# Linear attention into a GELU layer: the feature map as a minimum of two branches, and the first batch's v casts moved ahead

## The chip, the cores and the metric

The kernel runs on one core of a Trainium2 chip. The metric is the device time of one execution in microseconds (us). The engines of the core run side by side and meet through semaphores: TensorE (PE; its weight loads are listed as PEld), VectorE (DVE), ScalarE (ACT), GpSimd (POOL) and SyncE (SP), which here only issues DMA transfers.

## The reference

Two parts follow one another. The first is linear attention over 8 batches and 8 heads, with 576 tokens and 64 features a head; the second is a two-layer network with a tanh-approximated GELU over all 4608 tokens (512 to 2048 to 512 features).

```
def phi(x):
    return np.where(x > 0, x, np.exp(x) - 1.0) + 1.0
q_p, k_p = phi(q), phi(k)
kv  = np.einsum('bhsd,bhse->bhde', k_p, v)
z   = np.sum(k_p, axis=2)
num = np.einsum('bhsd,bhde->bhse', q_p, kv)
den = np.einsum('bhsd,bhd->bhs', q_p, z)[..., None] + 1e-06
x   = (num / den), tokens x (heads * 64)
h   = x @ w_in
g   = 0.5 * h * (1.0 + np.tanh(c * (h + 0.044715 * h * h * h)))
out = g @ w_out
```

The feature map phi is exp(x) for x up to 0 and x + 1 above. Everything is given and returned in 32-bit floats; the kernel multiplies in bf16.

## The kernel before

**Tiling.** The 576 tokens of a batch are 512 "main" tokens, on 128 partitions with C = 4 tokens ("chunks") in each, and 64 "rest" tokens; the rests of two batches share one tile. q, k and v of a batch are loaded as fp32 tiles of 128x2048 in the order head, chunk, feature (`load_main`, line 63). For the matrix products the feature map's result is wanted in the order chunk, head, feature (`k_p`, `q_p`), so that two heads of one chunk are a block of 128 columns.

**Feature map.** ACT writes e = exp(x) in bf16, in the order of the load (`exp_main`, lines 164 to 167; for the first batch and its rests line 341 and `exp_rest_half`). DVE then clamps e to 1 in place (line 171) and computes max(x, 0) + e for each of the four chunks, with the result in chunk order (`phi_into`, lines 169 to 178). `phi_of`, `phi_rest` and `phi_rest_half` are the same for whole tiles, whole rests and half a rest.

**Attention of a batch.** v is cast to bf16 next to a column of ones (`cast_v`, line 202, and `cast_vr`, line 208). `kv_mm` (line 213) sums kv and z over the chunks and the rest in PSUM; `kv_evac` (line 234) copies them out to a block-diagonal tile `kvbd`. q_p is transposed: on PE for the first two batches (`transpose_q`, line 332, and `tq`, line 555), by DMA transposes issued by SP for the others (lines 455 and 608). `nab_mm` (line 251) multiplies by `kvbd`, `nab_evac` divides, and the result x is transposed again into `xt`.

**Network.** For each batch j, `first_half` makes 16 blocks m of h on PE (`first_mm`, line 298, 4 products each) with GELU on ACT, and `second_half` (line 703) makes the output on PE (line 718, 64 products), which ACT or DVE copy out. A ninth turn handles the rests of all batches.

**Order.** The order on every engine is written out by hand. The prologue (lines 339 to 405) does batch 0 step by step; `keep_warm` issues products on a zero tile so that PE stays busy. From then on `at(half, j, slot, fn)` puts the preparation of later batches between the products of earlier ones.

**Weights and buffers.** Loads of q, k, v and of the weights share one pool of six fp32 buffers (`pld`, tag `ld`), so a load waits until the buffer's former tile has been read. SP issues them in one queue: k and q of batch 0, the first half of the k and v rests, v of batch 0, the first two quarters of w_in, k of batch 1, the rest of w_in, then w_out in four blocks with q and v of batch 1 between them. POOL casts w_in (line 149) and most of w_out (line 156) to bf16 after they land. The second half of j = 0 takes the output tiles in turns, so that its first 16 products need only the first block of w_out.

**The lines that matter for the prologue.** The exps of k and q by halves of the heads (line 341), their maps (line 346), four transposes and copies of q (ACT, lines 348 and 354), the v casts, and the kv products in two groups h of four heads. Before group 0, ACT casts heads 0 to 3 of v; between the groups, DVE casts heads 4 and 5 and ACT heads 6 and 7 (lines 357 to 359).

Of the kernel before, what the change touches and what calls it, by code (L numbers as in the profile page):

```python
# [9 lines left out]
BF16 = mybir.dt.bfloat16  # L10
AF = mybir.ActivationFunctionType
ALU = mybir.AluOpType
# [3 lines left out]
def kernel(  # L16
# [12 lines left out]
    nc = tc.nc  # L29

    B, H, S, D = q.shape
    d_model, d_ff = moe_w_in.shape
    P = 128
    C = 4
# [12 lines left out]
    pe = ctx.enter_context(tc.tile_pool(name="pe", bufs=1))  # L47
# [52 lines left out]
    ld = {}  # L100
# [43 lines left out]
    def gelu_table():  # L144
        nc.scalar.preload_act_table_set("gelu_apprx_tanh_and_others")  # L145
# [15 lines left out]

    phi = {}

    def exp_main(name, b):
        e = pe.tile([P, H, C * D], BF16, name=name + "_e")
        nc.scalar.activation(e, ld[name, b], AF.Exp)  # L166
        return e

    def phi_into(xp, x, e, hs):

        nc.vector.tensor_scalar(e[:, hs], e[:, hs], 1.0, None, op0=ALU.min)  # L171
        xv = x.rearrange("p h (c d) -> p c h d", d=D)
        ev = e.rearrange("p h (c d) -> p c h d", d=D)
        for c in range(xp.shape[1]):
            nc.vector.scalar_tensor_tensor(  # L175
                xp[:, c, hs, :], xv[:, c, hs, :], 0.0, ev[:, c, hs, :],
                op0=ALU.max, op1=ALU.add,
            )

    def phi_of(x, e, name):  # L180
        xp = pphi.tile([P, x.shape[2] // D, H, D], BF16, name=name)
        phi_into(xp, x, e, slice(0, H))
        return xp

    def phi_rest(name, m):
        x = ld[name, m]
        e = pe.tile([P, H, D], BF16, name=f"{name}_e{m % 2 if name == 'qr' else ''}")
        nc.scalar.activation(e, x, AF.Exp)
        return lambda: phi.__setitem__((name, m), phi_of(x, e, name + "_p"))

    def exp_rest_half(name, e, s):
        r = slice(REST * s, REST * (s + 1))
        nc.scalar.activation(e[r], ld[name, 0][r], AF.Exp)

    def phi_rest_half(name, e, s):
        r = slice(REST * s, REST * (s + 1))
        nc.vector.tensor_scalar(e[r], e[r], 1.0, None, op0=ALU.min)
        nc.vector.scalar_tensor_tensor(
            phi[name, 0][r, 0], ld[name, 0][r], 0.0, e[r], op0=ALU.max, op1=ALU.add
        )  # L200

    def cast_v(b, fn, s=slice(0, H)):
        fn(  # L203
            out=vps[b % 2][:, s, :, 0:D],
            in_=ld["v", b][:, s].rearrange("p h (c d) -> p h c d", d=D),
        )

    def cast_vr(m, halves=(0, 1)):
        for s in halves:
            r = slice(REST * s, REST * (s + 1))  # L210
            nc.vector.tensor_copy(out=vrs[m % 2][s][r, :, 0:D], in_=ld["vr", m][r])

    def kv_mm(b, i, kv_ps, at_i=None):
        i_ps = i if at_i is None else at_i
        kp = phi["k", b].rearrange("p c h d -> p c (h d)")
        kr = phi["kr", b // 2].rearrange("p c h d -> p c (h d)")
        dst = kv_ps[:, i_ps // 2, 2 * E * (i_ps % 2) : 2 * E * (i_ps % 2) + 2 * E]
        for c in range(C):
            nc.tensor.matmul(  # L219
                dst,  # L220
                lhsT=kp[:, c, P * i : P * (i + 1)],
                rhs=vps[b % 2][:, 2 * i : 2 * i + 2, c, :],
                start=(c == 0),
                stop=False,
            )
# [70 lines left out]
    gs, hs = {}, {}  # L296
# [18 lines left out]
    ke = pe.tile([P, H, C * D], BF16, name="k_e")  # L315
    qe = pe.tile([P, H, C * D], BF16, name="q_e")
    kre = pe.tile([P, H, D], BF16, name="kr_e")
# [7 lines left out]
    def keep_warm(n):  # L325
        w_ps = ps_ho.tile([P, 512], FP32, name="w_ps", tag="ho")
        for _ in range(2 * n):
            nc.tensor.matmul(w_ps[:, 0:252], lhsT=warm[:, 0:P], rhs=warm)  # L328

    halves = (slice(0, 4), slice(4, 8))  # L330

    def transpose_q(i, copy):
        src = q_src(0)
        t_ps = ps_ho.tile([P, C, 2, P], BF16, name="t_ps", tag="ho")
        for c in range(C):
            nc.tensor.transpose(t_ps[:, c, 0, :], src(c, i), ident)
        copy(out=qt[:, :, i, :], in_=t_ps[:, :, 0, :])

    for n, e in (("k", ke), ("q", qe)):
        for s in halves:  # L340
            nc.scalar.activation(e[:, s], ld[n, 0][:, s], AF.Exp)
    exp_rest_half("kr", kre, 0)
    keep_warm(36)
    for n, xp, e in (("k", kp, ke), ("q", qp, qe)):
        for s in halves:
            phi_into(xp, ld[n, 0], e, s)
    for i in range(2):
        transpose_q(i, nc.scalar.copy)
# [44 lines left out]
    keep_warm(1)  # L393
    tx0(1)
    ke1 = exp_main("k", 1)
    kre1 = pe.tile([P, H, D], BF16, name="kr_e")
    exp_rest_half("kr", kre1, 1)
    gelu_table()
    nab0(3)
# [122 lines left out]
    def plan_second():  # L522

        b = 1
        box = {}

        def exps():
            box["q"] = pe.tile([P, H, C * D], BF16, name="q_e")
            for s in halves:
                nc.scalar.activation(box["q"][:, s], ld["q", b][:, s], AF.Exp)  # L530
            gelu_table()

        def phis():
            phi["q", b] = pphi.tile([P, C, H, D], BF16, name="q_p")
            for s in halves:
                phi_into(phi["q", b], ld["q", b], box["q"], s)
# [257 lines left out]
```

## Time and profile before

| what | value |
|---|---|
| median of four runs | 297.69 us (295.9 to 298.21) |
| the profiled execution, own time | 297.55 us |
| its span, first to last instruction | 295.8 us |
| granted TensorE clock | 1.000 |
| PE busy | 285.7 us, 97% |
| ACT busy | 159.7 us, 54% |
| DVE busy | 130.1 us, 44% |
| POOL busy | 37.1 us, 13% |
| DVE clamp, 128x2048 (line 171) | 13 times, 811 ns (k) and 689 ns (q) on average |
| DVE max and add, 128x512 (line 175) | 28 for k at 746 ns, 24 for q at 686 ns |
| ACT exp, 128x2048 (line 166) | 13 times, about 1.9 us |
| DVE cast of v, 128x2048 (line 203) | 7 times, 1223 ns |
| first FFN product begins | 21.28 us |

A busy share is an average over the whole span. Which engine sets the end is read from the chain of waits and from the list of who waited for whom; idle time of an engine that nobody waits for costs nothing. Matmuls are pipelined, so that their single durations overlap: 64 products of 128x512 take about 13.8 us of PE, not 64 times the 379 ns listed for one.

### The profile page before, as it was taken

What the parts mean: (1) busy time and instruction counts of PE and PEld (TensorE: products, weight loads), DVE (VectorE), ACT (ScalarE), POOL (GpSimd) and SP (SyncE); (2) the same over time, 40 slices, a digit from 0 to 9 for tenths busy, and PEclk for the clock granted to TensorE, in tenths of its full rate; (3) what the DMA queues carried; (4) which work ended last, traced back from release to release, by engine and by line L of the source; (5) the groups of instructions that cost most, each with busy time, mean ns of one, the idle gap of its engine ahead of it and who ended that gap; (6) DMA issues with size and microseconds to landing.
All of it is one profiled execution on the core that took longest, in us unless ns stands there. A gap on an engine that the chain in (4) does not pass through costs nothing.

```text
span 295.8 us, 4289 instructions
## 1 busy us (share of the span) xinstructions
PE 285.7 (97%) x1669; PEld 149.2 (50%) x1698; DVE 130.1 (44%) x244; ACT 159.7 (54%) x222; POOL 37.1 (13%) x56
## 2 busy tenths in 40 slices
PE   8979999999999999999999999999999999999995
PEld 6756445644565444544455445544544444444443
DVE  2868555327689578244624493437142000000002
ACT  4649943579955762658256935683551066017500
POOL 8046567500001500000000000000000000000000
PEclk9999999999999999999999999999999999999999
DMA  7999999993399999637924696203331110021032
GB/s 246 330 365 406 397 371 379 299 371 109 83 319 285 170 299 322 159 74 231 334 90 68 203 335 144 53 20 112 100 55 36 71 71 2 0 86 56 2 71 72
DMA packets 64260, 53.24 MB, mean 180 GB/s; under 512 B 31728, under 2 KB 57584, under 8 KB 64240
## 3 DMA queue, kind: packets, MB, share of 16 engines
q1 hardware_dynamic: 60816, 41.82, 49.3%
q10 hardware_dynamic: 2464, 8.52, 7.4%
q0 software_dynamic: 960, 2.62, 3.8%
q8 instruction: 13, 0.21, 0.3%
q14 instruction: 7, 0.06, 0.1%
HBM read 36.70 MB, written 9.44 MB: 156 GB/s over the span
## 4 chain that ended last, share of the span: by engine, by line
PE 79%; DMA 12%; DVE 4%; issue 2%; ACT 1%; SPq 0%; POOL 0%; DVEq 0%
PE o_ps L718 39%; PE h_ps L301 33%; DMA w_st<-in_moe_w_out_dram 4%; DMA q_x<-in_q_dram 3%; DMA w_st<-in_moe_w_in_dram 3%; PE n_ps L253 3%; PE kv_ps L219 2%; DMA qt<-q_p 2%; PE o_ps L687 1%; DVE q_p L175 1%; DVE kvbd L242 1%; DVE k_p L175 1%; PE t_ps L276 1%; PE kv_ps L226 1%; SPq L67 0%
## 5 line engine op out<-in xcount | busy, mean ns | idle before, releaser
L718 PE MATMUL o_ps<-w_out_sb,g 128*128 128x512 bf16 x545 | 123.7, 379 | 1.2 <-POOL w_out_sb L156 0.4
L301 PE MATMUL h_ps<-xt,w_in_sb 128*128 128x512 bf16 (+1 forms) x535 | 118.8, 364 | 0.8
L675 ACT ACTIVATE g<-h_ps 128x512 bf16<-128x512 f32 x144 | 83.8, 598 | 47.8 <-PE h_ps L301 45.2
L718 PEld LDWEIGHTS <-g 128*128 128x128 bf16 x560 | 54.1, 98 | 63.2 <-issue 0.7
L301 PEld LDWEIGHTS <-w_in_sb 128*128 128x128 bf16 x612 | 57.7, 98 | 54.7 <-issue 0.5
L733 ACT COPY o_sb<-o_ps 128x512 f32<-128x512 f32 x18 | 10.6, 586 | 57.1 <-PE o_ps L718 56.8
L731 DVE COPY o_sb<-o_ps 128x512 f32<-128x512 f32 x17 | 11.7, 688 | 62.4 <-PE o_ps L718 62.3
L265 DVE TENSOR_TENSOR x<-n_ps,r 128x512 bf16<-128x512 f32 x36 | 24.9, 692 | 1.2
L175 DVE SCALAR_TENSOR_TENSOR k_p<-k_x,k_e 128x512 bf16<-128x512 f32 (+1 forms) x36 | 22.0, 674 | 0.3
L175 DVE SCALAR_TENSOR_TENSOR q_p<-q_x,q_e 128x512 bf16<-128x512 f32 (+1 forms) x40 | 21.5, 601 | 0.3
L242 DVE CAST kvbd<-kv_ps 64x260 bf16<-64x260 f32 (+1 forms) x16 | 6.6, 410 | 28.3 <-PE kv_ps L226 28.2
L263 DVE RECIPROCAL r<-n_ps 128x8 f32<-128x8 f32 x36 | 7.4, 206 | 25.3 <-PE n_ps L253 25.3
L171 DVE TENSOR_SCALAR k_e<-k_e 128x2048 bf16<-128x2048 bf16 (+1 forms) x9 | 6.6, 731 | 23.7 <-ACT k_e L166 19.1
L328 PE MATMUL w_ps<-warm 128*128 128x252 bf16 x94 | 13.3, 304 | 1.1 <-DVE warm L127 1.1
L253 PEld LDWEIGHTS <-qt 128*128 128x128 bf16 x128 | 9.7, 98 | 8.7 <-issue 1.1
L301 PE MATMUL h_ps<-xt_rest,w_in_sb 128*128 128x512 bf16 x63 | 13.9, 379 | 0.1
L253 PE MATMUL n_ps<-kvbd,qt 128*128 128x130 bf16 x128 | 12.7, 221 | 1.2 <-DMA qt<-q_p 0.6
L166 ACT ACTIVATE k_e<-k_x 128x2048 bf16<-128x2048 f32 x7 | 13.4, 1911 | 0.4 <-DMA k_x<-in_k_dram 0.4
L219 PEld LDWEIGHTS <-k_p 128*128 128x128 bf16 x128 | 9.7, 97 | 6.8 <-issue 1.4
L203 DVE CAST vp<-v_x 128x2048 bf16<-128x2048 f32 (+1 forms) x8 | 9.0, 1122 | 9.3 <-DMA v_x<-in_v_dram 9.3
L219 PE MATMUL kv_ps<-vp,k_p 128*128 128x130 bf16 x128 | 12.2, 220 | 0.9 <-DVE vp L203 0.8
L145 ACT ACT_TABLE_LOAD x8 | 10.3, 1283 | 3.8 <-DVE o_sb L731 3.8
(58 smaller groups left out, 147.4 us busy)
## 6 DMA issues: line engine op xcount, KB each, us to landing
out_dram<-o_sb ACTq DMA_DIRECT2D x16, 512.0 KB, 3.6
k_x<-in_k_dram SPq DMA_DIRECT2D x7, 1024.0 KB, 6.0
v_x<-in_v_dram SPq DMA_DIRECT2D x7, 1024.0 KB, 12.1
q_x<-in_q_dram SPq DMA_DIRECT2D x6, 1024.0 KB, 9.3
w_st<-in_moe_w_out_dram SPq DMA_DIRECT2D x4, 1024.0 KB, 11.7
w_st<-in_moe_w_in_dram SPq DMA_DIRECT2D x3, 1024.0 KB, 8.8
q_x<-in_q_dram SPq DMA_DIRECT2D x4, 512.0 KB, 10.3
k_x<-in_k_dram SPq DMA_DIRECT2D x2, 512.0 KB, 4.2
```

The lines of the kernel that those rows point to most:

```text
L145: nc.scalar.preload_act_table_set("gelu_apprx_tanh_and_others")
L166: nc.scalar.activation(e, ld[name, b], AF.Exp)
L175: nc.vector.scalar_tensor_tensor(xp[:, c, hs, :], xv[:, c, hs, :], 0.0, ev[:, c, hs, :], op0=ALU.max, op1=ALU.add,)
L219: nc.tensor.matmul(dst, lhsT=kp[:, c, P * i : P * (i + 1)], rhs=vps[b % 2][:, 2 * i : 2 * i + 2, c, :], start=(c == 0), stop=False,)
L253: nc.tensor.matmul(n_ps[rows, i // 2, 2 * E * (i % 2) : 2 * E * (i % 2) + 2 * E], lhsT=qt_c[:, i, rows], rhs=kvbd[:, i, :], skip_group_che ...
L265: nc.vector.tensor_tensor(x, n_v[:, :, :, 0:D], r[:, :, :, None].to_broadcast([P, 2, 4, D]), op=ALU.mult,)
L301: nc.tensor.matmul(h_ps[:, tok], lhsT=w_in_sb[:, c, P * m : P * (m + 1)], rhs=xt[:, c, tok], start=(c == 0), stop=(c == KM - 1), skip_grou ...
L328: nc.tensor.matmul(w_ps[:, 0:252], lhsT=warm[:, 0:P], rhs=warm)
L675: nc.scalar.activation(gs[j][:, i, :], ps, AF.Gelu_apprx_tanh)
L718: nc.tensor.matmul(o_pss[t], lhsT=g[:, m, P * t : P * (t + 1)], rhs=w_out_sb[:, m, :], start=(m == 0), stop=(m == MM - 1),)
L731: nc.vector.tensor_copy(dst, o_ps)
L733: nc.scalar.copy(dst, o_ps)
```

## The change

The feature map is written as min(exp(x), max(x + 1, 1)), which is the same function: below 0 the maximum is 1 and exp is smaller; above 0 exp(x) is larger than x + 1. Each map is now two DVE operations over all chunks instead of one clamp and an operation per chunk: `phi_line` computes max(x + 1, 1) from the loaded fp32 tile and writes bf16 in chunk order, and `phi_min` takes the minimum with e, in place. So that both inputs of the minimum lie in the same order, ACT writes exp in chunk order (`exp_into`), and the tiles for e have the shape chunk, head, feature.

In the prologue, ACT's cast of v's heads 0 to 3 and the casts between the two kv groups are replaced by four casts ahead of both groups: DVE takes heads 0, 1, 4 and 5, ACT heads 2, 3, 6 and 7. The copy of the last transposed block of q (i = 3) goes from ACT to DVE. The first call of `keep_warm` issues 66 products instead of 72.

```
+    def by_chunk(x):
+        return x.rearrange("p h (c d) -> p h c d", d=D)
+
+    def exp_into(e, x, hs=slice(0, H)):
+        nc.scalar.activation(
+            e[:, :, hs, :].rearrange("p c h d -> p h c d"), by_chunk(x[:, hs]), AF.Exp
+        )
+
     def exp_main(name, b):
-        e = pe.tile([P, H, C * D], BF16, name=name + "_e")
-        nc.scalar.activation(e, ld[name, b], AF.Exp)
+        e = pe.tile([P, C, H, D], BF16, name=name + "_e")
+        exp_into(e, ld[name, b])
         return e

-    def phi_into(xp, x, e, hs):
-
-        nc.vector.tensor_scalar(e[:, hs], e[:, hs], 1.0, None, op0=ALU.min)
-        xv = x.rearrange("p h (c d) -> p c h d", d=D)
-        ev = e.rearrange("p h (c d) -> p c h d", d=D)
-        for c in range(xp.shape[1]):
-            nc.vector.scalar_tensor_tensor(
-                xp[:, c, hs, :], xv[:, c, hs, :], 0.0, ev[:, c, hs, :],
-                op0=ALU.max, op1=ALU.add,
-            )
+
+    def phi_line(xp, x, hs=slice(0, H)):
+        nc.vector.tensor_scalar(
+            xp[:, :, hs, :].rearrange("p c h d -> p h c d"), by_chunk(x[:, hs]),
+            1.0, 1.0, op0=ALU.add, op1=ALU.max,
+        )
+
+    def phi_min(xp, e, hs=slice(0, H)):
+        nc.vector.tensor_tensor(
+            xp[:, :, hs, :], xp[:, :, hs, :], e[:, :, hs, :], op=ALU.min
+        )
...
     def phi_rest_half(name, e, s):
         r = slice(REST * s, REST * (s + 1))
-        nc.vector.tensor_scalar(e[r], e[r], 1.0, None, op0=ALU.min)
-        nc.vector.scalar_tensor_tensor(
-            phi[name, 0][r, 0], ld[name, 0][r], 0.0, e[r], op0=ALU.max, op1=ALU.add
-        )
+        phi_line(phi[name, 0][r], ld[name, 0][r])
+        phi_min(phi[name, 0][r], e[r])
...
     for n, e in (("k", ke), ("q", qe)):
         for s in halves:
-            nc.scalar.activation(e[:, s], ld[n, 0][:, s], AF.Exp)
+            exp_into(e, ld[n, 0], s)
     exp_rest_half("kr", kre, 0)
-    keep_warm(36)
+    keep_warm(33)
     for n, xp, e in (("k", kp, ke), ("q", qp, qe)):
         for s in halves:
-            phi_into(xp, ld[n, 0], e, s)
+            phi_line(xp, ld[n, 0], s)
+            phi_min(xp, e, s)
     for i in range(2):
         transpose_q(i, nc.scalar.copy)
     keep_warm(5)
     phi_rest_half("kr", kre, 0)
-    cast_v(0, nc.scalar.copy, halves[0])
     cast_vr(0, (0,))
     for i in range(2, NP):
-        transpose_q(i, nc.scalar.copy)
+        transpose_q(i, nc.scalar.copy if i == 2 else nc.vector.tensor_copy)
     keep_warm(2)
     for h in range(2):
-        if h == 1:
-            cast_v(0, nc.vector.tensor_copy, slice(4, 6))
-            cast_v(0, nc.scalar.copy, slice(6, 8))
+        cast_v(0, nc.vector.tensor_copy, slice(4 * h, 4 * h + 2))
+        cast_v(0, nc.scalar.copy, slice(4 * h + 2, 4 * h + 4))
+    for h in range(2):
         kv_ps = ps_a.tile([P, 2, 512], FP32, name="kv_ps", tag="a")
         for i in range(2):
             kv_mm(0, 2 * h + i, kv_ps, i)
...
```

`phi_of`, `phi_rest`, `exp_rest_half` and the exps and maps of batch 1's q call the new functions in the same way.

More of the change, by code (lines that the diff above doesn't have):

```diff
@@ L162 @@
     phi = {}
+    def by_chunk(x):
[4 more added lines that the diff above has]
+        )
     def exp_main(name, b):
-        e = pe.tile([P, H, C * D], BF16, name=name + "_e")
-        nc.scalar.activation(e, ld[name, b], AF.Exp)
-        return e
-    def phi_into(xp, x, e, hs):
-        nc.vector.tensor_scalar(e[:, hs], e[:, hs], 1.0, None, op0=ALU.min)
-        xv = x.rearrange("p h (c d) -> p c h d", d=D)
-        ev = e.rearrange("p h (c d) -> p c h d", d=D)
-        for c in range(xp.shape[1]):
-            nc.vector.scalar_tensor_tensor(
-                xp[:, c, hs, :], xv[:, c, hs, :], 0.0, ev[:, c, hs, :],
-                op0=ALU.max, op1=ALU.add,
-            )
+        e = pe.tile([P, C, H, D], BF16, name=name + "_e")
+        exp_into(e, ld[name, b])
+        return e
+    def phi_line(xp, x, hs=slice(0, H)):
[7 more added lines that the diff above has]
+        )
     def phi_of(x, e, name):
         xp = pphi.tile([P, x.shape[2] // D, H, D], BF16, name=name)
-        phi_into(xp, x, e, slice(0, H))
+        phi_line(xp, x)
+        phi_min(xp, e)
         return xp
@@ L186, in phi_rest @@
         x = ld[name, m]
-        e = pe.tile([P, H, D], BF16, name=f"{name}_e{m % 2 if name == 'qr' else ''}")
-        nc.scalar.activation(e, x, AF.Exp)
+        e = pe.tile([P, 1, H, D], BF16, name=f"{name}_e{m % 2 if name == 'qr' else ''}")
+        exp_into(e, x)
         return lambda: phi.__setitem__((name, m), phi_of(x, e, name + "_p"))
@@ L192, in exp_rest_half @@
         r = slice(REST * s, REST * (s + 1))
-        nc.scalar.activation(e[r], ld[name, 0][r], AF.Exp)
+        exp_into(e[r], ld[name, 0][r])
     def phi_rest_half(name, e, s):
         r = slice(REST * s, REST * (s + 1))
-        nc.vector.tensor_scalar(e[r], e[r], 1.0, None, op0=ALU.min)
-        nc.vector.scalar_tensor_tensor(
-            phi[name, 0][r, 0], ld[name, 0][r], 0.0, e[r], op0=ALU.max, op1=ALU.add
-        )
+        phi_line(phi[name, 0][r], ld[name, 0][r])
+        phi_min(phi[name, 0][r], e[r])
     def cast_v(b, fn, s=slice(0, H)):
@@ L313, in first_mm_early @@
         first_mm(j, m, hs[j, m], slice(0, MAIN // 2))
-    ke = pe.tile([P, H, C * D], BF16, name="k_e")
-    qe = pe.tile([P, H, C * D], BF16, name="q_e")
-    kre = pe.tile([P, H, D], BF16, name="kr_e")
+    ke = pe.tile([P, C, H, D], BF16, name="k_e")
+    qe = pe.tile([P, C, H, D], BF16, name="q_e")
+    kre = pe.tile([P, 1, H, D], BF16, name="kr_e")
     kp = pphi.tile([P, C, H, D], BF16, name="k_p")
@@ L395 @@
     ke1 = exp_main("k", 1)
-    kre1 = pe.tile([P, H, D], BF16, name="kr_e")
+    kre1 = pe.tile([P, 1, H, D], BF16, name="kr_e")
     exp_rest_half("kr", kre1, 1)
@@ L527, in exps @@
         def exps():
-            box["q"] = pe.tile([P, H, C * D], BF16, name="q_e")
+            box["q"] = pe.tile([P, C, H, D], BF16, name="q_e")
             for s in halves:
-                nc.scalar.activation(box["q"][:, s], ld["q", b][:, s], AF.Exp)
+                exp_into(box["q"], ld["q", b], s)
             gelu_table()
@@ L535, in phis @@
             for s in halves:
-                phi_into(phi["q", b], ld["q", b], box["q"], s)
+                phi_line(phi["q", b], ld["q", b], s)
+                phi_min(phi["q", b], box["q"], s)
         def cast_vs():
```

## The prediction

> **What bounds the kernel now.** I read the page's busy shares first, then the chain of waits in order of time, then TensorE's own waits, then the table of stretches and the timeline at the two places where the chain leaves TensorE. TensorE (PE) is busy for 97% of the span, and this sets the scale: a faster VectorE (DVE, 44%) can bring nothing except where PE waits. The chain (start, length, what) leaves PE for long in two places. This is the first:
>
> ```profile
> 16.93 0.39 PE kv_ps L219 x4
> ...
> 17.40 8.13 DMA w_st<-in_moe_w_in_dram
> 25.53 12.54 DMA w_st<-in_moe_w_out_dram
> 38.12 1.25 POOL w_out_sb L156
> 39.41 3.61 PE o_ps L718 x16
> ```
>
> The prologue's attention ends its kv products at 17.4 us; from there the chain runs through weight loads until PE goes on at 39.41. PE is not idle all this time: from 21.28 it computes the first half of batch 0's FFN. PE's waits (total, times, longest) say how much it lost:
>
> ```profile
> PE kv_ps L219 <- DVE vp L203: 0.8, 1, 0.8
> PE n_ps L253 <- DMA qt<-q_p: 0.6, 1, 0.6
> PE t_ps L276 <- DVE x L265: 0.6, 2, 0.4
> PE o_ps L718 <- POOL w_out_sb L156: 0.4, 1, 0.4
> ```
>
> The first and third lie in the prologue; the fourth (0.44 us before 39.41) and the second (0.59 us before 101.84) lie behind transfers. The stretches show what the early transfers are bound by (stretch and its length; PE, PEld, DVE, ACT, POOL busy; clock; DMA share; GB/s):
>
> ```profile
> 28.00:30.00 2.00, 2.00 (x11) 0.92 (x10) 1.97 (x2) 1.85 (x5) 2.00 (x2) 1.00 1.05 394
> 38.00:40.00 2.00, 1.56 (x8) 0.62 (x7) 1.63 (x3) 1.39 (x3) 1.88 (x2) 1.00 1.09 366
> 130.00:140.00 10.00, 9.95 (x52) 4.46 (x52) 4.85 (x10) 7.18 (x8) 0.00 (x0) 1.00 0.63 181
> ```
>
> In steps of half a microsecond the DMA share is never under 1.00 from 6 to 42 us: the 16 engines are full, so the second w_out block lands near 38.1 however early the engines are. After 105 us PE is full too (9.95 of 10).
>
> **What the Trainium skill says.** "VectorE: DVE Perf Modes", section on the perf-mode tier table: over 2048 elements in SBUF an fp32 `tensor_scalar` takes 1227 ns and a bf16 `tensor_tensor` 1224 ns. The trace agrees on one-input fp32 work (the v casts, 1223 ns); it has no bf16 `tensor_tensor` from SBUF. "SBUF — State Buffer", section Who interferes with whom: GpSimd (POOL) and a DVE operation with two SBUF inputs, or in a two-port mode, block each other. The trace agrees: four k_p operations took 4.18 us from 25.08 beside POOL casts, and 2.50 us from 86.85 with POOL idle. "TensorE: Matmul & The Clock Gate", section Why this matters for your kernels: a PE gap of more than about 3 us lowers the clock. The granted clock here is 1.000; no gap so long occurs, so no trace shows it.
>
> **The change, part by part.**
>
> *Feature map.* For 128x2048 elements, before, one `tensor_scalar` and four `scalar_tensor_tensor`: the k of batch 3 holds DVE from 86.13 to 89.26, 3.13 us. After, an fp32 `tensor_scalar` (nearest row, the v cast: 1.22) and a bf16 `tensor_tensor`. For the latter I bound it by 0.69 us (the row of the bf16 `tensor_scalar`) and 2.33 us (one element at a time: 128x256 took 0.418 and 128x512 0.692, so 1.07 ns an element) and take the page's 1.22. With the 0.04 us that stand between dependent operations in the trace and the 0.08 us by which the next one overlaps, the sum is 1.22 + 0.04 + 1.22 - 0.08 = 2.40: 0.73 us less. There are 13 such maps, so some 9.5 us of DVE time; a rest's map (128x512) gains about 0.2. Nearly all of it lies beside a full PE and is worth nothing. The new first operation does not need exp, so it can run while exp does; the minimum then waits for exp as the old clamp did, with the same operations queued behind it.
>
> *Exp by chunk.* ScalarE (ACT) writes the same elements in runs of 64. The nearest row, its v cast with a gap after every 64, takes 1.05 us for 1024 against 1.057 for exp: cost 0. If scattered writing cost a tenth, two ACT exps would be 0.2 us longer in the prologue, hidden as what follows.
>
> *Prologue.* For 1024 elements I interpolate the DVE casts (0.411 at 512, 1.223 at 2048): 0.68 us for either new operation. The second half of q lands at 10.73; the line part runs to 11.43 while exp runs to 11.81, the minimum from 11.84 to 12.52. Before, q_p was done at 13.73: 1.2 us saved. Behind it on DVE: k's rest (2 x 0.41), the v rest cast 0.41, the moved qt copy 0.42, two v casts of 0.41 each, so about 14.9. On ACT: the exps to 12.33, three copies to about 13.8, two v casts of 0.62 to about 15.0. The v casts, now all ahead of the kv copies, leave no wait between the two kv groups (before: 0.8 and 0.2 us of PE). The last kv product moves from 17.39 to about 15.7 and the first FFN product from 21.28 to about 19.6: 1.6 us, or 1.0 if the second half of v, first read at 15.86 in this trace, is late. Six warm-up matmuls less only let the transposes start earlier. The first w_in cast (17.26, about 1.0 us) is in time.
>
> *What is late next.* PE then asks for m = 6 and 8 at about 25.1 and 26.9. The w_in casts on POOL follow landings at about 23.4 and 25.9, and the DVE work on batch 1's k, now starting at about 23.0 rather than 23.5, can push one back by a two-port operation (1.2): PE loses some 0.4 us. It still comes to the end of the 16 products on the first w_out block at 38.97 - 1.6 + 0.4, about 37.8, and waits for the cast of the second block, which waits for its landing at 38.1. So the gain becomes a wait of about 1.4 us, up from 0.44. What is left of it: at 38.12 the POOL cast took 1.25 us beside DVE's q_p (37.36 to 39.63). The first half of q's line now runs before exp (34.01 to 36.01) and the map ends near 36.9, so the cast should take its undisturbed 1.04: minus 0.21 us.
>
> *Batch 3.* The second place in the chain:
>
> ```profile
> 89.35 1.14 DVE vp L203
> 90.49 0.61 DVE q_e L171
> ...
> 95.78 6.01 DMA qt<-q_p
> 101.84 0.41 PE n_ps L253 x4
> ```
>
> And SyncE's queue (SPq) in the timeline there:
>
> ```profile
> 91.88 5.12 SPq L455 DMA_TRANSPOSE qt<-q_p  x4
> ```
>
> Four DMA transposes issue back to back, 1.28 us each, the first when chunk 0 of q_p exists (91.12 + 0.69 = 91.81). After, all chunks come at once: 86.13 + 2.40 (k) + 1.14 (v cast, as in the chain) + 1.22 + 0.04 + 1.22 = 92.15. DVE is 0.7 us ahead after k and loses that by no longer handing over by chunk. The issues move by plus 0.3 us, and so does the landing at 101.79, on which PE waits. Bounds: with a 0.69 us minimum (k and q) minus 0.7 us, with 2.33 plus 2.5. Earlier batches transpose on PE or wait for kv; later ones have microseconds of room (SyncE from 114.17, PE asks at 123.7).
>
> *Sum*, against the profiled execution's own 297.55 us (span 295.8 and 1.75 around it): -0.2 + 0.3 = +0.1, so 297.6. The median of the four runs is 297.69, 0.14 above that execution.
>
> **The rivals.**
>
> *A, the prologue's gain is kept* (296.0): the second w_out block lands earlier with the rest. For it: SyncE's queue shows waits for slots ahead of w_out loads (1.8 us on a POOL cast, 1.3 us on k_p), which now end earlier. Against: the DMA share of at least 1.00; an earlier issue then only lengthens a queue. Sum: 297.55 - 1.6 + 0.1 = 296.05.
>
> *B, slower, by the minimum at one element per cycle*: 2.33 us instead of 1.22. Its place is batch 3, twice, ahead of the transposes; the price is 2 x 1.11 on top of the forecast, 299.8. It decides from the point where the minimum exceeds about 1.1 us, since the slack of qt is already negative. For: no row of this trace shows the fast form of an operation with two SBUF inputs. Against: both inputs are bf16 in dense runs, and the page prices just this.
>
> *C, the longer wait at 39 us cools PE's clock*: 1.4 to 2 us idle is under 3, but the waits of other engines could stretch it. An estimate from that page (section What's actually happening: an idle or busy window of about 3.4 us, half clock when cold): plus 1.7, 299.3.
>
> **How the numbers follow.** Forecast 0.58, A 0.20, B 0.14, C 0.08. What a measurement here can tell from no change is about 0.5%, 1.5 us. Of the forecast's 0.58, 0.54 lie within it and 0.02 on either side; so faster 0.22, same 0.54, slower 0.24. The range takes in A with a little below and C: 295.7 to 299.3; outside are B and the tails, under 0.2. The forecast's own range, from the bounds at batch 3 and the scatter of runs (295.9 to 298.21), is 296.4 to 298.6.
>
> **What would show it.** Right: the first FFN product on w_in near 19.6, PE's wait on w_out_sb grown to 1 to 2 us and ending near 39.2, the two new DVE operations near 1.2 us each for 2048, DVE's total down by about 10 us, PE's wait on qt still there. Wrong: a PE wait on w_out_sb that stays at 0.4 with everything after it earlier (A), a minimum of 2.3 us (B), a granted clock under 1.000 (C), or any PE wait after 105 us.

## The result, and the profile after

The changed kernel takes 297.32 us (median of 43 runs, 296.26 to 301.47), the kernel before 297.27 (64 runs, 295.42 to 299.49). The ratio is 1.0011, with an interval of 0.9997 to 1.0025: no change that can be told. Medians here are of all runs, while each ratio and its interval leave out the slow runs, those over 1.5% above the fastest of their kernel (two of these 43, five of the 22 of experiment 5). The profiled execution took 297.08 us, with a span of 295.3 and a granted clock of 1.000.

So there is a feature map that is a fifth shorter on VectorE (2.46 us from its start to the next operation in batch 3, before 3.13), and a prologue that is shorter by a microsecond and a half, and the time stays. Three questions follow: did the parts do what they should, where did the gain go, and can it be had?

The parts did. These are the groups of the new operations, by form (line, engine, operation, out<-in, count | busy us, mean ns | idle before):

```profile
L185 DVE TENSOR_TENSOR k_p<-k_p,k_e 128x2048 bf16<-128x2048 bf16 x7 | 9.1, 1299 | 12.3 <-ACT k_e L168 12.1
L179 DVE TENSOR_SCALAR k_p<-k_x 128x2048 bf16<-128x2048 f32 x7 | 8.5, 1220 | 0.9 <-DMA k_x<-in_k_dram 0.9
L185 DVE TENSOR_TENSOR q_p<-q_p,q_e 128x2048 bf16<-128x2048 bf16 x6 | 7.4, 1225 | 0.6
L179 DVE TENSOR_SCALAR q_p<-q_x 128x2048 bf16<-128x2048 f32 x6 | 7.3, 1222 | 0.1
```

Both operations take 1.22 us for 128x2048; only one minimum, beside POOL's casts, took 1.75 and lifts the mean for k to 1299. DVE's total fell from 130.1 to 114.6 us. ACT's exp by chunk takes 1.9 us for 2048 elements, as before.

The gain is seen in TensorE's timeline (start, length, what, idle before and its releaser), at the places where the prediction looked:

```profile
19.11 1.04 PE L309 MATMUL h_ps<-xt,w_in_sb 128*128 128x256 bf16 x8
...
27.00 7.08 PE L309 MATMUL h_ps<-xt,w_in_sb 128*128 128x512 bf16 x32 [0.56 <-POOL w_in_sb L149]
...
38.00 3.61 PE L727 MATMUL o_ps<-w_out_sb,g 128*128 128x512 bf16 x16 [0.47 <-POOL w_out_sb L156]
...
101.43 0.41 PE L261 MATMUL n_ps<-kvbd,qt 128*128 128x130 bf16 x4 [1.59 <-DMA qt<-q_p]
```

Before, PE went through the first half of the FFN without a wait that the view lists:

```profile
21.28 1.04 PE L301 MATMUL h_ps<-xt,w_in_sb 128*128 128x256 bf16 x8
...
22.37 13.14 PE L301 MATMUL h_ps<-xt,w_in_sb 128*128 128x256 bf16 x71
35.35 3.62 PE L718 MATMUL o_ps<-w_out_sb,g 128*128 128x512 bf16 x15
```

The third line of the first list stood at 39.41 and the last at 101.84. The lead is 2.17 us, then 1.41, then 0.41, and 0.5 in the span. Of the 2.17, 0.66 is not the change's: q's second half landed at 10.07 us rather than 10.73 (0.02 us before the start of its exp). This landing scatters between 9.27 and 11.66 over all kernels here, whose loads up to it are the same. From that landing to the first FFN product are 10.55 us before and 9.04 after, so the change brought 1.51 us. What took it is in PE's waits (total, times, longest):

```profile
PE n_ps L261 <- DMA qt<-q_p: 1.6, 1, 1.6
...
PE h_ps L309 <- POOL w_in_sb L149: 0.6, 1, 0.6
...
PE o_ps L727 <- POOL w_out_sb L156: 0.5, 1, 0.5
```

The wait on w_in is new (0.56), the one on w_out is what it was (0.47 against 0.44), and the wait on qt has grown from 0.59 to 1.59. So in these two executions the lead is lost at two gates, one on weights and one on a DMA transpose, some 60 us apart, both at the end of a transfer. The chain of waits names w_out and the transpose:

```profile
25.49 11.37 DMA w_st<-in_moe_w_out_dram
...
36.91 1.05 POOL w_out_sb L156
38.00 3.61 PE o_ps L727 x16
...
94.87 6.52 DMA qt<-q_p
...
101.43 0.41 PE n_ps L261 x4
```

The second w_out block lands at 36.86, 1.2 us before its old time, though its load is issued at the same time (25.49, before 25.53). So it did not hold PE to the old time. Of the 0.76 us that the first gate took (2.17 to 1.41), nearly all is w_in: from the first FFN product to the end of the 15 products on w_out PE needs 18.43 us, before 17.69.

The second gate is the odd one. The DVE work of batch 3 starts at 84.73 (before 86.13), so the lead is still 1.40. The first transpose is issued at 90.94 (91.88): lead 0.94. The last lands at 101.39 (101.79): lead 0.40. Half of the second loss is the handover of q_p as a whole, which the prediction priced; the other half is a longer flight. A transpose's time from issue to landing is the last line of the answer for the tile qt in this stretch. Before:

```profile
DMA to landing us min/median/max: 3.1/3.8/6.0
```

and after:

```profile
DMA to landing us min/median/max: 2.4/4.4/6.5
```

What else is under way there? GpSimd's queue loads the rest tokens for later batches (8 loads of 128 KB). Before:

```profile
95.09 1.36 POOL L76 DMA_DIRECT2D q_r<-in_q_dram  x2 [36.22 <-ACT g L675]
```

and after:

```profile
91.76 1.36 POOL L76 DMA_DIRECT2D q_r<-in_q_dram  x2 [34.42 <-DVE qr_p L185]
```

The first of them waits for the buffer of earlier q rests, and the queue behind it waits too. In the changed kernel its releaser is the map of q rests on DVE, which now ends at 91.68 us (before at 94.55, and there the record names an ACT operation as the last to be done). So the loads start 3.3 us earlier, among the transposes (issued from 90.94 to 96.1) rather than behind most of them. The first of them is read at 105.93 us, for batch 4. So a faster engine has released a transfer that nobody was waiting for, into the path of one that PE waits for. Whether this is what costs the time had to be tried.

### The profile page after: what moved, and what is told of

The parts are those of the page before. It is cut to its first block, busy times and chain, and to the rows that moved or that the text cites. A ratio compares the mean times of both kernels' runs of the same rounds, so it can differ in the third digit from the quotient of the medians.

```text
span 295.3 us, 4211 instructions
## 1 busy us (share of the span) xinstructions
PE 284.6 (96%) x1663; PEld 148.2 (50%) x1692; DVE 114.6 (39%) x189; ACT 158.7 (54%) x221; POOL 36.0 (12%) x56
## 4 chain that ended last, share of the span: by engine, by line
PE 81%; DMA 10%; SPq 4%; ACT 1%; DVE 1%; issue 1%; POOL 0%; ACTq 0%
PE o_ps L727 39%; PE h_ps L309 35%; DMA w_st<-in_moe_w_out_dram 4%; DMA k_x<-in_k_dram 4%; PE n_ps L261 3%; DMA qt<-q_p 2%; PE kv_ps L227 2%; SPq L67 2%; PE o_ps L696 1%; SPq L463 1%; SPq L90 1%; ACT k_e L168 1%; PE t_ps L284 1%; SPq L76 1%; DVE kvbd L250 1%
## 5 line engine op out<-in xcount | busy, mean ns | idle before, releaser
L740 DVE COPY o_sb<-o_ps 128x512 f32<-128x512 f32 x17 | 11.7, 689 | 64.5 <-PE o_ps L727 64.5
L168 ACT ACTIVATE k_e<-k_x 128x2048 bf16<-128x2048 f32 (+1 forms) x9 | 15.5, 1721 | 5.6 <-DMA k_x<-in_k_dram 5.5
L168 ACT ACTIVATE q_e<-q_x 128x2048 bf16<-128x2048 f32 (+1 forms) x10 | 15.6, 1560 | 2.5 <-DMA q_x<-in_q_dram 2.5
L185 DVE TENSOR_TENSOR k_p<-k_p,k_e 128x2048 bf16<-128x2048 bf16 (+1 forms) x9 | 10.5, 1164 | 12.8 <-ACT k_e L168 12.5
L336 PE MATMUL w_ps<-warm 128*128 128x252 bf16 x88 | 12.5, 305 | 1.2 <-DVE warm L127 1.1
L211 DVE CAST vp<-v_x 128x2048 bf16<-128x2048 f32 (+1 forms) x9 | 9.4, 1044 | 10.3 <-DMA v_x<-in_v_dram 10.3
L179 DVE TENSOR_SCALAR q_p<-q_x 128x2048 bf16<-128x2048 f32 (+1 forms) x10 | 10.7, 1068 | 5.7 <-DMA q_x<-in_q_dram 5.6
L179 DVE TENSOR_SCALAR k_p<-k_x 128x2048 bf16<-128x2048 f32 (+1 forms) x9 | 10.4, 1153 | 4.4 <-DMA k_x<-in_k_dram 4.4
## 6 DMA issues: line engine op xcount, KB each, us to landing
w_st<-in_moe_w_out_dram SPq DMA_DIRECT2D x4, 1024.0 KB, 11.7
```

The lines of the kernel that those rows point to most:

```text
L168: nc.scalar.activation(e[:, :, hs, :].rearrange("p c h d -> p h c d"), by_chunk(x[:, hs]), AF.Exp)
L179: nc.vector.tensor_scalar(xp[:, :, hs, :].rearrange("p c h d -> p h c d"), by_chunk(x[:, hs]), 1.0, 1.0, op0=ALU.add, op1=ALU.max,)
L185: nc.vector.tensor_tensor(xp[:, :, hs, :], xp[:, :, hs, :], e[:, :, hs, :], op=ALU.min)
L740: nc.vector.tensor_copy(dst, o_ps)
```

## The experiments

Two theories stood at first. *Two gates*: the prologue's gain is real, part of it is taken at the weights and the rest at the qt transposes, which fly longer beside the rest loads. *Handover*: the loss at batch 3 lies on DVE, since q_p is complete only after its minimum over all chunks. Later the question moved to which gate takes how much, and to what the warm-up products do. One profile was kept for each kernel, so a wait in it is that of one execution; where the text goes from a wait to the time of many runs, the ratio has to carry it. Every ratio is against the kernel before, run on the same chip with it.

**1. The rest loads out of the transposes' way, with the change.** The loads for batches 4 and 5 (q) and 6 and 7 (k, v and q) go to SP's queue, where they come behind the transposes:

```
-    def load_rests(m, names):
+    def load_rests(m, names, eng=nc.gpsimd):
...
-            ld[n, m] = load_rest(src, m, n[0] + "_r", nc.gpsimd)
+            ld[n, m] = load_rest(src, m, n[0] + "_r", eng)
...
-        at(2, 2 * m - 3, 3, lambda m=m: load_rests(m, (("kr", k), ("vr", v))))
-        at(1, 2 * m - 2, 9, lambda m=m: load_rests(m, (("qr", q),)))
+        eng = nc.sync if m == 3 else nc.gpsimd
+        at(2, 2 * m - 3, 3, lambda m=m, e=eng: load_rests(m, (("kr", k), ("vr", v)), e))
+        at(1, 2 * m - 2, 9, lambda m=m: load_rests(m, (("qr", q),), nc.sync))
```

> The changed kernel, with the rest loads of q for batches 4 and 5 and of k, v and q for batches 6 and 7 issued by SyncE in their planned places instead of by GpSimd, which runs ahead and issues them at 91.8 to 97.2 us, beside batch 3's DMA transposes. Theory 'two gates' (the prologue's gain of some 2 us is real, PE loses 0.5 us of it to the w_in cast at 27, 0.5 to the second w_out block at 38 and the rest to the landing of batch 3's last transpose, which the rest loads make late): the last transpose lands within about 4 us of its issue instead of 6.5, PE's wait on qt falls from 1.6 to under 0.3 us, and the time is 1.0 to 1.8 us under the kernel before (ratio 0.994 to 0.997). Rival 'handover' (the wait comes from q_p being handed over whole, so that the transposes are issued late): the wait stays over 1.0 us and the ratio is 0.999 to 1.002.

Measured: 295.33 us (17 runs), 0.9966 [0.9943, 0.9988], span 293.1: as *two gates* expected. The transposes' flight is now

```profile
DMA to landing us min/median/max: 2.4/2.4/2.4
```

and PE waits for qt no longer. The stretch from 92 to 96 us shows the same (stretch; PE, PEld, DVE, ACT, POOL; clock; DMA share; GB/s), first of the changed kernel, then of this one:

```profile
92.00:96.00 4.00, 3.95 (x23) 1.99 (x23) 1.96 (x4) 2.35 (x5) 4.00 (x7) 1.00 0.97 206
```

```profile
92.00:96.00 4.00, 3.95 (x23) 1.99 (x23) 1.71 (x4) 2.39 (x4) 0.00 (x0) 1.00 0.43 97
```

The DMA share falls from 0.97 to 0.43, with the same transposes in it. The handover is as whole as in the changed kernel, and the wait is gone: as the main cause of the wait it falls. That the rest loads lengthen the flight is shown, and the second gate with it. That their earlier start made it longer than before (6.5 rather than 6.0 us at most) is read from two traces and was not tried by itself, since this run takes the loads away altogether and changes their queue too.

**2. The same on the kernel before** (the same edit).

> The kernel before with the same shift of the rest loads to SyncE. Two gates: PE's wait on qt (0.59 us in its profile) vanishes, 0.3 to 0.7 us less time, ratio 0.9975 to 0.999; the difference to the changed kernel with the same shift is then the prologue's gain that survives the weight loads, 0.5 to 1.4 us. Handover: no change of the wait or of the time.

Measured: 297.5 us (14 runs), 1.0016 [0.999, 1.0042]. The wait on qt is gone here too, and yet the time is not lower: a miss. In its profile DVE's last copy comes 1.07 us earlier than before (291.08 against 292.15), but the span ends 4.6 us after that copy begins and not 3.7: the output's last two transfers land 2.9 and 3.0 us after their issue rather than 2.1 and 2.2. Such an end is seen only here and in run 11, both with the old map and these loads moved; why is open. So this run is a poor measure of what the edit is worth by itself, and a part of what runs 1, 6 and 7 gain on the kernel before may be the edit's. Ahead of the end the two kernels with the edit can be compared. PE's last product of batch 3 on qt begins here at

```profile
100.78 0.40 PE L253 MATMUL n_ps<-kvbd,qt 128*128 128x130 bf16 x4
```

and in run 1 at

```profile
99.26 0.40 PE L261 MATMUL n_ps<-kvbd,qt 128*128 128x130 bf16 x4
```

From q's landing that is 89.77 and 88.34 us. With the second gate open, 1.4 of the 1.6 us that run 1's prologue is shorter in these two profiles are still there at batch 3.

**3. The map alone** (casts, copies and warm-up as before).

```
-    keep_warm(33)
+    keep_warm(36)
...
+    cast_v(0, nc.scalar.copy, halves[0])
...
-        transpose_q(i, nc.scalar.copy if i == 2 else nc.vector.tensor_copy)
+        transpose_q(i, nc.scalar.copy)
...
-        cast_v(0, nc.vector.tensor_copy, slice(4 * h, 4 * h + 2))
-        cast_v(0, nc.scalar.copy, slice(4 * h + 2, 4 * h + 4))
-    for h in range(2):
+        if h == 1:
+            cast_v(0, nc.vector.tensor_copy, slice(4, 6))
+            cast_v(0, nc.scalar.copy, slice(6, 8))
```

> The changed kernel with the casts of v, the copies of q and the 72 warm-up products as before: the feature map alone. Both theories: the first FFN product at about 19.9 to 20.4 us (from 21.28; the map saves 1.2 us of it, the casts the rest), DVE busy about 115 us. Two gates: PE's waits at the weight loads and at qt take it up, ratio 0.998 to 1.002. Handover: with less head start and the same late issue, slower than before by 0.3 to 0.6 us, ratio 1.001 to 1.002.

Measured: 297.9 us (22 runs), 1.0029 [1.001, 1.0048], slower by a hair and above both expected ranges, though the interval reaches into them. From q's landing to the first FFN product it takes 10.04 us: half a microsecond is won, not one and a half. PE waits 0.36 us for ACT's cast of v ahead of the first kv group, and 0.78 and 0.15 for the casts between the groups, as before. PE's wait on qt is 1.19; on the weights it does not wait in this execution.

**4. The casts alone** (the old map; exp in the order of the load; the casts, the copy and the warm-up as in the change).

```
-    def phi_line(xp, x, hs=slice(0, H)):
...
-    def phi_min(xp, e, hs=slice(0, H)):
...
+    def phi_into(xp, x, e, hs):
+        nc.vector.tensor_scalar(e[:, hs], e[:, hs], 1.0, None, op0=ALU.min)
...
+            nc.vector.scalar_tensor_tensor(
+                xp[:, c, hs, :], xv[:, c, hs, :], 0.0, ev[:, c, hs, :],
+                op0=ALU.max, op1=ALU.add,
+            )
```

> The kernel before with the four v casts ahead of both kv groups, the last q copy on VectorE and 66 warm-up products: the casts alone. First FFN product at about 20.4 to 20.9 us. Two gates: the 0.5 to 0.8 us are taken up by the wait for the second w_out block and by qt, ratio 0.998 to 1.001. Handover: q_p still goes over by chunk, so what survives the weight loads stays, ratio 0.997 to 0.999.

Measured: 297.99 us (22 runs), 1.0033 [1.0014, 1.0051]: both expectations missed. From q's landing to the first FFN product it takes 11.06 us, half a microsecond more than before. PE's timeline and the stretches with the clock say why:

```profile
16.59 0.41 PE L219 MATMUL kv_ps<-vp,k_p 128*128 128x130 bf16 x4 [1.04 <-DVE vp L203]
```

```profile
14.00:16.00 2.00, 1.34 (x11) 0.77 (x11) 1.97 (x6) 1.22 (x4) 0.00 (x0) 1.00 1.05 405
16.00:18.00 2.00, 1.41 (x16) 1.42 (x17) 1.15 (x4) 0.56 (x2) 0.17 (x1) 0.73 1.08 386
18.00:20.00 2.00, 1.97 (x18) 1.68 (x16) 0.50 (x2) 0.53 (x2) 2.00 (x3) 0.50 1.09 371
```

With the old map DVE comes late to the v casts, PE stands for 1.04 us, and then the granted clock falls to 0.50. Neither part alone makes the time better. In the prologue they bring +0.5 us (casts, clock included) and -0.5 us (map), and -1.5 together.

**5. The minimum by chunks, with the change** (q_p of batches 2 to 7), which hands over by chunk as before:

```
-        phi_min(xp, e)
+        if name == "q_p":
+            for c in range(C):
+                phi_min(xp[:, c : c + 1], e[:, c : c + 1])
+        else:
+            phi_min(xp, e)
```

> The changed kernel, but for the q of batches 2 to 7 the minimum is taken chunk by chunk (four operations of 128x512 instead of one of 128x2048), so that the transposes can start on chunk 0; the rest loads stay with GpSimd. The first transpose should be issued about 0.9 us earlier relative to the map's start (about 5.3 us after it instead of 6.2). Theory 'handover': batch 3's last transpose lands as much earlier, PE's wait on qt falls from 1.6 to about 0.7 us, ratio 0.997 to 0.999. Theory 'rest loads' (the flight of the last transpose is long because GpSimd's rest loads are on the same DMA engines): the landing follows by less than half of the 0.9 us, the wait stays at 1.1 us or more, ratio 0.9995 to 1.002.

Measured: 297.38 us (22 runs), 0.9976 [0.9951, 1.0001]. The first transpose is issued 5.42 us after the start of k's map, 0.8 us sooner than the 6.21 of the changed kernel. But PE still waits 1.26 us for qt, and the longest flight is now 6.8 us. Counted from the start of k's map the last transpose lands 0.3 us sooner, so only 0.3 of the 0.8 arrived. By the wait the rest loads decide. The ratio says otherwise: it lies in the range of *handover*, its interval reaches into the other one, and the median of all 22 runs is that of the kernel before beside them (297.39). It does not settle the question.

**6. The map alone with the rest loads moved** (edits 1 and 3).

> The feature map alone (casts, copies and warm-up as before) with the rest loads moved to SyncE as in the first run. Rest loads: no wait on qt; from the landing of q's second half to the first FFN product 10.0 us as in the map-alone run, against 8.9 with the casts moved, so about 1.0 us over the first run and 0.3 to 0.8 under the kernel before, ratio 0.997 to 1.000. Rival 'weights take it' (what the prologue gains is taken by the landing of the w_in and w_out blocks): the same time as the first run within 0.3 us, ratio 0.9955 to 0.9975.

Measured: 296.12 us (22 runs), 0.9959 [0.994, 0.9979]. By the ratio this is what run 1 gave with the whole change (0.9966), as *weights take it* expected. But neither profile shows that mechanism: PE runs through the place of the first gate without a listed wait, in run 1

```profile
20.95 13.14 PE L309 MATMUL h_ps<-xt,w_in_sb 128*128 128x256 bf16 x71
33.93 7.10 PE L727 MATMUL o_ps<-w_out_sb,g 128*128 128x512 bf16 x31
```

and here

```profile
21.79 13.14 PE L309 MATMUL h_ps<-xt,w_in_sb 128*128 128x256 bf16 x71
34.77 7.07 PE L728 MATMUL o_ps<-w_out_sb,g 128*128 128x512 bf16 x31
```

In these two executions run 1 leads by 0.83 us at the first FFN product and still by 0.7 at the end (spans 293.1 and 293.8). So edit 1 and the map alone go with 0.4%; whether the casts add to it stays open, since each interval is some 0.6 us wide to either side.

**7. Both edits, with the change.** Edit 1, and the second w_out block is loaded ahead of q of batch 1, which opens the w_out part of the first gate (the w_in loads stay as they are); q's exps move by four slots, since q then lands later:

```
+    wo_st.append(load_w_out(1))
...
-    wo_st += [load_w_out(i) for i in (1, 2)]
+    wo_st.append(load_w_out(2))
...
-        at(1, 0, 11, exps)
+        at(1, 0, 15, exps)
```

> The first run's kernel with the second w_out block loaded ahead of batch 1's q, and batch 1's exps after the last GELU of batch 0's first half. The second block should land about 2.6 us earlier, so that PE cannot wait on it. Weights take it: 0.4 to 0.8 us faster than the first run, ratio 0.994 to 0.9955. Rest loads (the weight loads take at most some tenths once the transposes don't hold): within 0.4 us of the first run, ratio 0.9955 to 0.998.

Measured: 294.99 us (7 runs), 0.9909 [0.9877, 0.9941], span 292.4: better than either expectation. PE's waits on w_in, w_out and qt are all gone; its timeline runs through the place of the first gate without a break:

```profile
23.78 9.66 PE L309 MATMUL h_ps<-xt,w_in_sb 128*128 128x512 bf16 x43
33.27 7.07 PE L728 MATMUL o_ps<-w_out_sb,g 128*128 128x512 bf16 x31
```

This profile is of the fastest of the seven executions. Its span is 0.7 us shorter than that of run 1, and q's second half landed 0.88 us earlier in it, while run 1 waited for no weights either. So what the w_out edit adds to run 1 stands in the ratios (0.9909 and, in run 12, 0.9916, against 0.9966); the profiles don't show how.

**8. The casts alone with more warm-up** (run 4, with 12 products rather than 4 ahead of kv):

```
-    keep_warm(2)
+    keep_warm(6)
```

> The casts alone with 12 warm-up products instead of 4 ahead of the kv products. Theory 'cold clock' (the casts alone came out slow because PE waited 1.0 us for v at 15.6 and its granted clock fell to 0.50 from about 17 to 20 us): the clock stays at 1.00 and the first FFN product comes 10.3 to 10.7 us after the landing of q's second half instead of 11.1. Rival (VectorE's longer queue alone delays it): 11.0 or more.

Measured (a single execution): the first FFN product comes 10.21 us after q's landing, against 11.06 in run 4 (a little sooner than the 10.3 to 10.7 expected), and the clock holds:

```profile
16.00:18.00 2.00, 1.76 (x27) 1.51 (x25) 0.67 (x3) 0.53 (x2) 1.30 (x2) 1.00 1.09 384
18.00:20.00 2.00, 1.63 (x21) 1.07 (x19) 1.90 (x6) 0.59 (x1) 1.71 (x2) 1.00 1.12 360
```

The first kv product comes 4.98 us after q's landing in both runs, so the whole 0.85 us lies behind it, where the clocks differ: it is the price of the cold clock, and eight idle products bought it back. With the clock held, the casts alone bring the prologue 0.3 us (10.21 against 10.55).

**9. The change with more warm-up** (`keep_warm` of 36 and 4 in place of 33 and 2).

> The changed kernel with 72 warm-up products at the start instead of 66 and 8 instead of 4 ahead of the kv products. Theory 'cold clock' (the shorter prologue leaves PE so little to do that its granted clock falls to 0.50 for some 3 us in those executions in which q's second half lands late; this took 1 us in the chunk run's profile and makes the changed kernel's upper tail, 10 of 43 runs over 298.6 us against 4 of 64 before): the tail shrinks to under one run in ten over 298.6, the median falls by 0.2 to 0.6 us under the kernel before (ratio 0.998 to 0.9995). Rival (the tail comes from transfers alone): the same tail and a ratio of 0.9995 to 1.002.

Measured: 297.04 us (22 runs), 0.9989 [0.9969, 1.0009]. Over 298.6 us lie 2 of its 22 runs, and 10 of 43 of the changed kernel (4 of 64 before). That fits a changed kernel which falls cold in the prologue in some executions, as run 5 did in its profile (0.50 from about 15 to 18 us). The mean clock on record for each run supports it: the profiled executions of runs 4 and 5, which fell cold, have 0.994 and 0.992. So low a mean (0.994 or less) have 7 of the 43 runs of the changed kernel, 5 of them among the 10 over 298.6, but only 5 of the 157 runs of the kernel before that were measured beside the experiments, and 1 of the 22 here. The other 5 of the 10 have 0.997 or more and are not explained, and that the products lower the median is not shown, since the interval includes 1.

**10. Only the w_out edit, with the change** (that of run 7, the rest loads as they were).

> The changed kernel with only the load order altered: second w_out block ahead of batch 1's q, batch 1's exps after the last GELU of the first half; the rest loads stay with GpSimd. Two gates in a row: PE no longer waits on w_out_sb, but what is gained there waits for batch 3's last transpose instead (wait on qt 1.5 to 2.5 us), ratio 0.998 to 1.0005. Rival (the weight loads are the one gate, the rest loads do little): ratio 0.993 to 0.996.

Measured: 297.69 us (14 runs), 0.9992 [0.9963, 1.002]. No wait on w_out is left, but PE waits 1.10 us for qt, and for w_in in this execution twice:

```profile
25.09 1.90 PE L309 MATMUL h_ps<-xt,w_in_sb 128*128 128x512 bf16 x8 [0.47 <-POOL w_in_sb L149]
27.66 7.08 PE L309 MATMUL h_ps<-xt,w_in_sb 128*128 128x512 bf16 x32 [0.67 <-POOL w_in_sb L149]
```

So the wait on qt is shorter than expected, and the ratio is in the range of *two gates*. The w_out edit alone brings nothing, together with edit 1 it goes with 0.9%. In this execution, however, little passed the first gate: w_in took 1.14 us, and PE is done with its first 31 products on w_out at 41.49, where the changed kernel was at 41.45.

**11. Both edits, without the change** (the edits of run 7 on the kernel before).

> The kernel before, without the change, with both gates taken away: rest loads on SyncE, and the second w_out block ahead of batch 1's q. Two gates: without the change the prologue is 1.5 us longer, and with no gate behind it this shows: 1.0 to 1.8 us over the changed kernel with the same two edits (ratio 0.9909 there), so ratio 0.995 to 0.998. Rival (the change is worth nothing wherever the transfers stand): ratio 0.990 to 0.993.

Measured: 298.81 us (22 runs), 1.0064 [1.0045, 1.0084], slower: both expectations missed. The later q of batch 1 meets the old map. In DVE's timeline:

```profile
39.39 3.11 DVE L175 SCALAR_TENSOR_TENSOR q_p<-q_x,q_e 128x256 bf16<-128x256 f32 x4
...
42.87 1.43 DVE L175 SCALAR_TENSOR_TENSOR q_p<-q_x,q_e 128x256 bf16<-128x256 f32 x4
```

Four operations take 3.11 us while POOL casts w_out, and 1.43 when it does not; PE then waits 0.93 us for q_p at 43.35, where there was no wait before. In run 7 the same map looks so:

```profile
34.72 1.30 DVE L179 TENSOR_SCALAR q_p<-q_x 128x1024 bf16<-128x1024 f32 x1 [8.15 <-DMA q_x<-in_q_dram]
36.96 0.69 DVE L185 TENSOR_TENSOR q_p<-q_p,q_e 128x1024 bf16<-128x1024 bf16 x1 [0.94 <-ACT q_e L168]
...
38.36 0.69 DVE L185 TENSOR_TENSOR q_p<-q_p,q_e 128x1024 bf16<-128x1024 bf16 x1
```

Its first operation does not wait for exp, so the map is done at 39.05, with time in hand. Between the kernel before with these edits and the changed one with them lie 1.5% (1.0064 against 0.9909), but that is not the worth of the change alone. The two profiles are 4.4 us apart (spans 296.8 and 292.4): 0.6 is q's landing, 1.6 the shorter prologue, which is all still there at batch 3, 0.9 the new wait on q_p, and 1.1 the longer end as in run 2, which is not explained; 0.2 is left over.

**12. Both edits, with the change and more warm-up** (the edits of runs 7 and 9).

> The changed kernel with both gates taken away and the warm-up products of the first run of this set: the version that should beat both. Cold clock and two gates together: ratio 0.990 to 0.993, with no run over 298. If the warm-up delays the prologue instead, 0.3 us over the run with both gates away alone.

Measured: 295.22 us (7 runs, 293.93 to 295.61), 0.9916 [0.9886, 0.9946]. The same as run 7, within the range expected. These two are the fastest kernels of the study, by their ratios 0.8 to 0.9% under the kernel before.

## Why the prediction was right

The forecast was that the prologue's gain is lost before the end, +0.1 us in all, and it was. But it named one main place for the loss, the wait on w_out, and that place did not take it. One of its own signs of being wrong even appeared at 38 us: PE's wait on w_out stayed at 0.4 to 0.5, and all behind it came 1.4 us earlier, until batch 3. That the sum still came out is luck. In the two profiles it can be redone from q's landing on: -1.51 (prologue) + 0.76 (weights, 2.17 to 1.41) + 0.46 (handover) + 0.54 (flight) = +0.25, on a lead of 0.66 that q's landing happened to give. This is the bookkeeping of one pair of executions; with a later landing the gates would have taken less. By its steps:

- **Map.** 1.22 for each operation, right to a hundredth. In batch 3 the minimum starts 0.10 us after its line ends rather than 0.04, so the handover cost 0.46 rather than 0.3. DVE's total fell by 15.5 us, not 10. By groups of instructions, the 13 whole maps went from 44.0 to 32.3, some 11.7 rather than 9.5, since the forecast took one undisturbed map and the old operations beside POOL were longer; the half maps of batches 0 and 1, which the 10 left out, brought 2.8, and the rests 1.8. (The groups add up to a little more than the total, in which operations that overlap count once.)
- **Exp by chunk.** No cost, as said.
- **Prologue.** 1.6 us forecast, 1.5 measured. It is more than its parts: the map alone brings 0.5 (run 3), the casts alone lose 0.5 (run 4), or gain 0.3 when the clock is held (run 8). The prediction worked out the two together and did not see this, nor that six warm-up products less are part of a prologue in which the clock can fall.
- **w_in.** 0.4 forecast; 0.56 measured as one wait, and some 0.7 with the slower stretch around it. It varies with the landings: none in run 1, 1.1 us in run 10.
- **w_out.** The term that was mis-sized. A wait of 1.4 us was forecast, with the block landing at 38.1 however early the engines are; it landed at 36.86, and the wait was 0.47, no more than before. The prediction took the landing of one execution for a fixed time, by the argument of a full DMA share. Over the ten profiles with this load order the cast of that block begins between 35.74 and 38.12, latest in the one that the prediction read, and PE waits for it in two of them, before and after. The POOL cast did fall from 1.25 to 1.05 us, as forecast.
- **Batch 3.** The other mis-sized term, with the opposite sign: +0.3 forecast, +1.0 measured. The 0.46 of handover was in the forecast; the 0.54 of flight was not. The prediction moved the DVE work and SP's queue, but not GpSimd's queue, which the same DVE work releases. Run 1 shows that these loads make the wait. The two errors, 0.9 us too much at w_out and 0.7 too little here, nearly cancelled.

Of the rivals, A (the gain kept) would have needed the second gate open: run 1, with it open, reached 0.9966, run 7 with both edits 0.9909. B is refuted by the 1.22 us. C named the right mechanism at the wrong place: the clock held at 39 us, but it fell in the prologue, in runs 4 and 5 and by the mean clocks in some of the changed kernel's executions, after much shorter gaps than the prediction allowed.

## What to carry to other kernels

When a gain is won early, follow the lead through the two profiles, place by place, until it is gone: there may be several gates in a row, and then opening one of them can show nothing (run 10), another a part (run 1), and both more (run 7). Before a landing is taken as a gate, look at several executions: it may be later in the one you read than in all the others. Ask of every engine that becomes faster which queues wait for the buffers it frees: an unhurried load can lengthen the flight of a transfer on the path. And two parts of a change that bring little or harm alone can bring more together; test them apart, and together, before you drop one.

## What was not expected of the hardware

- **The clock can fall after short gaps.** The Trainium skill, "TensorE: Matmul & The Clock Gate", section Why this matters for your kernels, speaks of gaps of more than about 3 us. Here a gap of 1.04 us in run 4, in a stretch in which PE had little work, was followed by a granted clock of 0.73 and 0.50 in the next two stretches of 2 us; run 5 fell so as well after gaps of 1.27 and 0.53. Eight small products in the gap kept it at 1.00 (run 8). But no threshold comes out of these runs: in run 3 a gap of 1.06 us, followed by a stretch in which PE was busy for little more than half of the time, left the clock at 1.00:

```profile
11.62 0.62 PE L344 MATMUL t_ps<-ident,q_p 128*128 128x128 bf16 x8 [1.06 <-DVE q_p L185]
```

```profile
16.00:18.00 2.00, 1.10 (x14) 0.95 (x14) 0.78 (x3) 1.00 (x3) 0.03 (x1) 1.00 1.08 380
```

  So in sparse work a gap of one microsecond can be enough and need not be; what decides stays open. Another section of the page, A second HAM failure mode: psum-queue depth-cycling, has a clock that swings because PE idles briefly but often between groups of products, which is nearer to what is seen here.
- **A transpose's flight depends on its company.** 2.4 us for each of the four in run 1, up to 6.5 beside the rest loads in the changed kernel and 6.8 in run 5; the DMA share beside the rest loads is 0.97 at only 206 GB/s.
- **DVE operations with two SBUF inputs suffer beside POOL, the new minimum among them.** 3.11 against 1.43 us for the old ones, 1.75 against 1.22 for the minimum; this agrees in kind with the Trainium skill, "SBUF — State Buffer", section Who interferes with whom, by which a DVE operation with two SBUF inputs contends with GpSimd's reads of SBUF.
